# Round 0 of the triangular inverses in blocks of 16, and w_in read 512 columns at a time

## The chip, the cores and the metric

One core of a Trainium2 chip runs the whole program. The metric is the device time of one execution in microseconds (us). The core has a matrix engine (PE), a vector engine (DVE), a scalar engine (ACT), a slower vector engine (POOL) and a sequencer (SP) that issues the DMA transfers. Each engine works through its own instructions in the order in which the program holds them; semaphores make it wait for another engine or for a transfer.

## The reference

Three layers follow each other on 4 sequences of 768 tokens. The first is a delta-rule attention with 8 heads of 48:

```python
for t in range(S):
    y[:, :, t] = einsum('bhd,bhde->bhe', q_t, state)
    v_old = einsum('bhde,bhd->bhe', state, k_t)
    state = state + beta_t * outer(k_t, v_t - v_old)
```

The second is a gated MLP: `h = relu(x @ w_in)`, half of `h` is normalised, mixed over tokens with `w_spatial`, multiplied with the other half, and goes through `w_out`. The third turns that by `theta = x @ w_theta` into `x cos`, `x sin`, mixes each over tokens, adds, and applies `w_ch`. The weights come as 64-bit floats, and `w_in` is 384 x 1024.

## The kernel before

**The recurrence in chunks.** The kernel cuts each sequence into 12 chunks of 64 tokens, 48 chunks in all, which follow each other. Inside a chunk the tokens depend on each other through a strictly lower triangular 64 x 64 matrix per head (the gram matrix of the keys, masked and scaled by beta). With the inverse of one plus that matrix in hand, a chunk is a handful of small matmuls. `chain(g)` emits them: `ru` from the state (L754, L755), a subtraction `rt` on DVE (L758), `ru` again with the inverse from tile `GX` (L765, L766), the new state `s` (L781, L783), and the output `py` (L793, L794). The next chunk needs that state, so the chunks are one long chain.

**The inverses in rounds.** Eight chunks of 4 head pairs make a round: 32 matrices per partition group, inverted together by `invert(r)`. There are six rounds, and two `GX` tiles that take turns. `invert` cuts each 64 x 64 matrix into four 32 x 32 blocks. The two diagonal blocks are turned by a DVE transpose into a layout `un` with one matrix element per column (L624), inverted by substitution, one column `k` at a time from 30 down to 1, a multiply into `tmp` (L646) and an add into `un` (L654) each, and turned back twice, into `xt` (L659) and into `GX` (L662). The off-diagonal block is the product of three: matmuls `f2` (L680) and `f3` (L686) with copies between them, in four groups `h` of 8 matrices (two chunks each). Round 0 cuts the rows of each step into two interleaved halves, so that it has 59 multiplies and 59 adds; the other rounds have 30 and 30. Round r+2 can't start before round r's chunks have used their `GX`.

**The weights.** `f64_to_f32` loads the two 32-bit halves of each number and puts an f32 together with one ACT and four DVE instructions (L815 to L821); `split` makes a high and a low part of it (L827, L828). `load_w1` does this for `w_in` in 12 pieces of 256 columns, whose raw halves lie in buffers of the `vh` ring and whose result lies in the `vl` ring.

**The order.** All instructions are given to a planner (`Plan.run`) as tasks with options of engines, estimated durations, a priority (lower goes first) and dependences. It picks, for each engine, the task that can start first by its estimates, and among equals the one of lower priority; tasks marked `crit` can go ahead of earlier ones. The big matmuls of the MLP (recorded at L895, tile `m`) fill PE between the chain's small ones. So an edit in one place changes the order everywhere behind it.

In the printed functions, `A` adds a task, `pr` is its priority, and `o_dve`, `o_cpp`, `o_cps` and `o_pe` give its engines and estimates.

Of the kernel before, what the change touches and what calls it, by code (L numbers as in the profile page):

```python
# [361 lines left out]
def kernel(  # L362
# [113 lines left out]
    r_un = ring("pa", "un", [128, 32, 32], F32, 1)  # L476
# [17 lines left out]
    load(mask, lambda: mask.t, mask_c, 32768, -58)  # L494
# [117 lines left out]
    def invert(r, pr):  # L612

        gx, G = GXt[r % 2], GXc[r % 2]
        cr = r == 0
# [15 lines left out]
        ub = [Buf(tile_=un.t) for _ in sets]  # L631
        fin = [[] for _ in sets]
        heads = []
        for k in range(30, 0, -1):
            for half in (0, 1):
                for i, (c0, st) in enumerate(sets):
                    t0 = k + 1 + (k + 1 - c0) % st
                    m = len(range(t0, 32, st))
                    if m <= 0:
                        continue  # L640
                    if half == 0:
                        tmp = fin[i] = r_tmp.new()

                        def fa(e, k=k, t0=t0, st=st, m=m, tmp=tmp):
                            t3 = tmp.t[:, 0:m * k].rearrange("p (t s) -> p t s", s=k)
                            eng[e].tensor_tensor(out=t3, in0=un.t[:, k:k + 1, 0:k].to_broadcast([128, m, k]),  # L646
                                                 in1=un.t[:, t0:32:st, k:k + 1].to_broadcast([128, m, k]), op=ALU.mult)

                        dur = d_dve(m * k) if en == "DVE" else d_pool(m * k)
# [688 lines left out]
```

## Time and profile before

| what | value |
|---|---|
| median of 3 runs | 828.1 us (825.38 to 828.17) |
| profiled execution, its own time | 822.64 us |
| its span from first to last instruction | 820.9 us |
| busy share of PE, DVE, ACT, POOL | 89%, 76%, 42%, 20% |
| mean granted TensorE clock | 0.938 of full speed |

A row of the timeline gives the start of an instruction (or of a run of like ones, x their number), its duration, the engine, the source line and the shapes. DVE instructions overlap a little, since the next starts while the last one drains, so the cost of one on a busy DVE is the distance between two starts. A matmul on 32-bit floats is recorded as two passes, so 16 of them show as x32. "idle before" is the time in which the engine stood still, and what it waited for.

### The profile page before, as it was taken

What the parts mean: (1) busy time and instruction counts of PE and PEld (TensorE: products, weight loads), DVE (VectorE), ACT (ScalarE), POOL (GpSimd) and SP (SyncE); (2) the same over time, 40 slices, a digit from 0 to 9 for tenths busy, and PEclk for the clock granted to TensorE, in tenths of its full rate; (3) what the DMA queues carried; (4) which work ended last, traced back from release to release, by engine and by line L of the source; (5) the groups of instructions that cost most, each with busy time, mean ns of one, the idle gap of its engine ahead of it and who ended that gap; (6) DMA issues with size and microseconds to landing.
All of it is one profiled execution on the core that took longest, in us unless ns stands there. A gap on an engine that the chain in (4) does not pass through costs nothing.

```text
span 820.9 us, 21495 instructions
## 1 busy us (share of the span) xinstructions
PE 731.4 (89%) x8672; PEld 672.6 (82%) x8672; DVE 623.4 (76%) x1536; ACT 347.8 (42%) x769; POOL 162.1 (20%) x176
## 2 busy tenths in 40 slices
PE   5256468989999898999999999979999999999998
PEld 5245457777888777897878989979999999999997
DVE  5999998599999899999965574587575575556545
ACT  3536337445534463543754342264333332333321
POOL 2033523143322333401100100042110111111100
PEclk9755769799999999999999999989999999999999
DMA  7615614455577787678684610351021101002001
GB/s 224 207 53 154 192 58 142 119 149 166 154 224 232 208 261 201 174 234 254 185 227 128 213 43 26 109 161 46 26 75 35 27 30 54 27 26 84 1 1 58
DMA packets 84995, 102.39 MB, mean 125 GB/s; under 512 B 8993, under 2 KB 65569, under 8 KB 84897
## 3 DMA queue, kind: packets, MB, share of 16 engines
q1 hardware_dynamic: 84896, 101.03, 41.3%
q8 instruction: 68, 1.11, 0.6%
q14 instruction: 31, 0.25, 0.1%
HBM read 74.38 MB, written 22.41 MB: 118 GB/s over the span
## 4 chain that ended last, share of the span: by engine, by line
PE 57%; DVE 24%; DMA 10%; issue 3%; ACT 3%; SPq 2%; POOLq 0%; ACTq 0%; DVEq 0%
PE m L895 30%; PE y L895 19%; DVE tmp L646 5%; DVE un L654 4%; DMA xr<-xd 2%; DMA xd<-xs 2%; PE gp L588 2%; SPq L431 2%; DMA vk<-in_vkn_dram 2%; PE ru L765 1%; PE py L793 1%; DMA k<-in_vkn_dram 1%; DVE GX L599 1%; DMA kq<-pp 1%; PE m L1181 1%
## 5 line engine op out<-in xcount | busy, mean ns | idle before, releaser
L895 PE MATMUL m<-w,vh 128*128 128x256 f32 x576 | 111.1, 292 | 0.7 <-ACT uT L401 0.5
L895 PEld LDWEIGHTS m<-w,vh 128*128 128x128 f32 x576 | 89.0, 191 | 4.3 <-ACT uT L401 0.7
L895 PE MATMUL y<-wr,z 128*128 128x384 f32 x432 | 88.1, 343 | 0.0
L895 PE MATMUL y<-w,z 128*128 128x384 f32 x432 | 84.6, 339 | 0.0
L895 PE MATMUL m<-w,vl 128*128 128x256 f32 x288 | 81.2, 282 | 0.0
L895 PEld LDWEIGHTS y<-wr,z 128*128 128x128 f32 x432 | 77.3, 191 | 0.0
L895 PEld LDWEIGHTS y<-w,z 128*128 128x128 f32 x432 | 75.6, 188 | 0.0
L646 DVE TENSOR_TENSOR tmp<-un 128x30 f32<-128x30 f32 (+21 forms) x209 | 68.5, 339 | 0.8
L654 DVE TENSOR_TENSOR un<-un,tmp 128x30 f32<-128x30 f32 (+21 forms) x209 | 66.9, 331 | 0.9
L765 PE MATMUL ru<-rt,GX 64*64 64x48 f32 x384 | 34.8, 235 | 34.2 <-DVE rt L758 33.9
L765 PEld LDWEIGHTS ru<-rt,GX 64*64 64x64 f32 x384 | 28.6, 146 | 43.3 <-DVE rt L758 39.6
L1201 DVE TENSOR_SCALAR ni<-m 128x384 int32<-128x384 f32 x24 | 13.3, 555 | 57.6 <-PE m L895 57.5
L895 PEld LDWEIGHTS m<-w,vl 128*128 128x128 f32 x288 | 54.9, 191 | 0.0
L566 POOL TENSOR_TENSOR gm<-mask,ng 128x256 f32<-128x256 f32 x53 | 40.7, 774 | 53.6 <-DVE pp L609 18.5
L895 PE MATMUL m<-wo,gh 128*128 128x384 f32 x192 | 48.9, 335 | 1.6 <-DVE rr L1203 1.6
L730 POOL TENSOR_TENSOR vk<-vk,ng 128x384 f32<-128x384 f32 x28 | 28.6, 1024 | 104.8 <-DMA vk<-in_vkn_dram 72.9
L895 PE MATMUL m<-xTh,wih 128*128 128x256 f32 x144 | 46.6, 323 | 0.0
L401 ACT ACTIVATE x<-m 128x384 f32<-128x384 f32 x15 | 7.3, 488 | 86.9 <-PE m L895 86.9
L401 ACT ACTIVATE W<-ru 64x192 f32<-64x192 f32 x85 | 27.5, 324 | 36.4 <-PE ru L766 35.0
L895 PE MATMUL m<-xTl,wih 128*128 128x256 f32 x144 | 41.2, 286 | 0.0
L895 PE MATMUL m<-xTh,wil 128*128 128x256 f32 x144 | 41.0, 285 | 0.0
L588 PE MATMUL gp<-kg 48*64 48x128 f32 x512 | 38.1, 291 | 2.4 <-issue 2.4
(189 smaller groups left out, 2070.4 us busy)
## 6 DMA issues: line engine op xcount, KB each, us to landing
kq<-in_kqT_dram SPq DMA_DIRECT2D x96, 128.0 KB, 3.8
vk<-in_vkn_dram SPq DMA_DIRECT2D x48, 192.0 KB, 3.5
kg<-in_kqT_dram SPq DMA_DIRECT2D x32, 256.0 KB, 3.4
gd<-gt SPq DMA_DIRECT2D x24, 256.0 KB, 3.6
graw<-gd SPq DMA_DIRECT2D x24, 256.0 KB, 2.8
k<-in_vkn_dram SPq DMA_DIRECT2D x24, 192.0 KB, 3.1
xd<-xs SPq DMA_DIRECT2D x48, 96.0 KB, 2.8
xr<-xd SPq DMA_DIRECT2D x24, 192.0 KB, 3.3
```

What stands on the lines that cost most here:

```text
L401: nc.scalar.activation(out=out, in_=in_, func=func, **kw)
L431: return P.add(dma(nbytes), lambda e: nc.sync.dma_start(out=out_fn(), in_=src), reads, [(buf, part)], prio, extra=LOADLAT)
L566: eng[e].tensor_tensor(out=gm.t, in0=mask.t.unsqueeze(1).to_broadcast([128, HP, CH]), in1=ng_b[r].t[:, j, 1].unsqueeze(2).to_broadcast([12 ...
L588: mm(out=pv()[o:o + 64, hp, :], lhsT=kh, rhs=kg.t[i:i + D, :, hp, :] if fused else kh, start=True, stop=True)
L599: nc.vector.scalar_tensor_tensor(out=GXt[1][:, u0 + hp], in0=GXt[1][:, u0 + hp], scalar=ng_b[1].t[:, j, 1, hp:hp + 1], in1=mask.t, op0=ALU ...
L646: eng[e].tensor_tensor(out=t3, in0=un.t[:, k:k + 1, 0:k].to_broadcast([128, m, k]), in1=un.t[:, t0:32:st, k:k + 1].to_broadcast([128, m, k ...
L654: eng[e].tensor_tensor(out=un.t[:, t0:32:st, 0:k], in0=un.t[:, t0:32:st, 0:k], in1=t3, op=ALU.add)
L730: lambda e: eng[e].tensor_tensor(out=vk.t, in0=vk.t, in1=ng_b[r].t[:, j].unsqueeze(3).to_broadcast([128, 2, HP, D]), op=ALU.mult), [ng_b[r ...
L765: mm(out=pu.t[64:128, hp, :], lhsT=gx[64:128, u, :], rhs=rt.t[64:128, hp, :], start=True, stop=True)
L793: mm(out=PYt[0:48, hp, q:q + 64], lhsT=w[:, 0, hp, :], rhs=kq.t[:, 1, hp, :], start=True, stop=True)
L895: mm(out=view(), lhsT=a, rhs=c, start=(start and q == 0 and s_ == 0), stop=(stop and q == tot - 1 and s_ == 2))
L1201: P.add(o_dve(DM), lambda e: nc.vector.tensor_scalar(out=ni.t, in0=th(), scalar1=1.0 / TWO_PI, scalar2=None, op0=ALU.mult), [ps], [ni], pr ...
```

## The change

1. **Substitution in blocks of 16, round 0 alone** (`TWO = (0,)`). The steps run from k = 14 down to 1, on the two 16 x 16 diagonal blocks of each 32 x 32 block at once: one multiply and one add per step, 28 instructions. The interleaved halves are gone in round 0 too; each instruction follows the one before.
2. **The block between them by products.** Each 32 x 32 block then needs its own off-diagonal 16 x 16 block. For each of the four groups, 32 small matmuls `g1` (L692) multiply, ACT copies the result to `ct` with a scale of 0 or 1 per partition, 64 small matmuls `g2` (L698, L700) multiply again, and two DVE instructions `s1`, `s2` (L711, L715) merge the results into `GX` and `xt`. The zeros and ones are two new columns of the mask tile. `g1` and `g2` use a PSUM buffer of the ring `m`.
3. **Groups one after another.** In round 0 each group of two chunks has its own copies (L722) and its own clearing (L725, POOL), and the later three groups get priorities 0.4, 2.4 and 4.4, which stand just ahead of the chunks that need them.
4. **w_in in 6 pieces of 512 columns**, whose raw halves lie in the buffers of the `uT` ring.

```diff
-    r_un = ring("pa", "un", [128, 32, 32], F32, 1)
+    r_un = ring("pa", "un", [128, 33, 32], F32, 1)
...
-        sets = [(0, 1)] if not cr else [(0, 2), (1, 2)]
...
+        if two:
+            ub = (lambda: un.t.rearrange("p t s -> p (t s)").rearrange("p (b x) -> p b x", b=2)[:, :, 0:512]
+                  .rearrange("p b (t s) -> p b t s", s=32))
+        for k in range(14 if two else 30, 0, -1):
+            m = (15 if two else 31) - k
+            tmp = r_tmp.new()
+            n = m * k * (2 if two else 1)
+            def fa(e, k=k, m=m, tmp=tmp, n=n):
+                if two:
+                    u4, t4 = ub(), tmp.t[:, 0:n].rearrange("p (b t s) -> p b t s", b=2, s=k)
+                    eng[e].tensor_tensor(out=t4, in0=u4[:, :, k:k + 1, 0:k].to_broadcast([128, 2, m, k]),
+                                         in1=u4[:, :, k + 1:16, k:k + 1].to_broadcast([128, 2, m, k]), op=ALU.mult)
+                    return
...
+            A([(en, dur)], fa, [un], [tmp], pr + 0.001 * (31 - k), crit=cr)
+            A([(en, dur)], fb, [tmp], [un], pr + 0.001 * (31 - k), crit=cr)
...
+        step = MU if two else 32
+        for h0 in range(0, 32, step):
+            p1 = pr + 0.2 if h0 == 0 else r * RM + h0 / HP + GH
...
+                    def g1(e, v1=v1, u0=u0):
+                        for u in range(MU):
+                            for q in (0, 32, 64, 96):
+                                mm(out=v1()[q:q + 32, u, :], lhsT=gx[q:q + 16, u0 + u, 0:32], rhs=xt.t[q:q + 16, u0 + u, :],
+                                   start=True, stop=True, tile_position=(q, q))
+                    def g2(e, v2=v2, u0=u0, ct=ct):
+                        for u in range(MU):
+                            for q in (0, 32, 64, 96):
+                                mm(out=v2(0)[q:q + 32, u, :], lhsT=ct.t[q:q + 32, u, :], rhs=gx[q:q + 32, u0 + u, 16:32],
+                                   start=True, stop=True, tile_position=(q, q))
+                                mm(out=v2(1)[q:q + 32, u, :], lhsT=gx[q:q + 32, u0 + u, 0:32], rhs=ct.t[q:q + 32, u, 0:16],
+                                   start=True, stop=True, tile_position=(q, q))
+                    A(o_pe(620), g1, [xt, gu], [ps], p1, crit=cr, act=0.185, mode=3)
+                    A([("ACT", d_actp(32 * MU))], lambda e, v1=v1, ct=ct: act(ct.t, v1(), ACTF.Copy, scale=mask_t.t[:, CH + 1:CH + 2]),
+                      [ps, mask_t], [ct], p1, crit=cr, port=False)
+                    A(o_pe(1150), g2, [ct, gu], [(ps, True)], p1, crit=cr, act=0.2, mode=3)
...
+                    A(o_dve(16 * MU), s1, [ps, gu, mask_t], [un1], p1, crit=cr, port=False)
+                    A(o_dve(16 * MU), s2, [ps, xt, mask_t], [xn1], p1, crit=cr, port=False)
...
-    r_cvr = Ring(pools, "pm", [128, 256, 2], I32, "vh", 6)
+    r_cvr = Ring(pools, "pm", [128, DF, 2], I32, "uT", 3)
...
-                for c in (c0, c0 + 256):
-                    pr = (WP0 + 0.1 * n) if n < 6 else 0.5 + 0.3 * n
+                pr = (WP0 + 0.1 * n) if n < 3 else 0.5 + 0.6 * n
```

**How the order moves.** Three places in the engines' order follow. The first is DVE at the end of round 0's substitution. `un` is the layout with one element per column, `GX_108` round 0's matrices, `vl` a piece of w_in. Before, the last steps, the two transposes back and what follows:

```order
L646 TENSOR_TENSOR tmp<-un 128x30
L654 TENSOR_TENSOR un<-un,tmp 128x14x2
L654 TENSOR_TENSOR un<-un,tmp 128x15x2
L646 TENSOR_TENSOR tmp<-un 128x15 x2
L654 TENSOR_TENSOR un<-un,tmp 128x15 x2
L659 STREAM_TRANSPOSE xt_725<-un 128x32x32
L662 STREAM_TRANSPOSE GX_108<-un 128x32x32
L407 COPY GX_108<-GX_108 32x32x32
```

Now the same place:

```order
L643 TENSOR_TENSOR tmp<-un 128x52
L653 TENSOR_TENSOR un<-un,tmp 128x2x13x2
L643 TENSOR_TENSOR tmp<-un 128x28
L653 TENSOR_TENSOR un<-un,tmp 128x2x14
L667 STREAM_TRANSPOSE xt_571<-un 128x32x32
L665 STREAM_TRANSPOSE GX_108<-un 128x32x32
L542 TENSOR_SCALAR ss<-ss 128x32
L767 TENSOR_TENSOR kq<-gp,gm 64x256 x2
```

In the whole substitution 118 instructions became 28, the multiplies and adds now alternate, and the copy of `GX` no longer follows the transposes.

The second place is PE behind these transposes. `mg` and `m` are PSUM tiles, `ru` the chain's. Before, from the first `f2` (L680) to chunk 0 (L765):

```order
L680 MATMUL mg<-xt_725,GX_108 32x32 x16
L686 MATMUL mg<-GX_108,ct 32x32 x16
L680 MATMUL mg<-xt_725,GX_108 32x32 x16
L765 MATMUL ru<-rt,GX_108 64x48
L766 MATMUL ru<-rt,GX_108 64x48
```

Now, from the last of `g2`'s rows (L698, L700; 128 of these matmuls stand here one by one, behind a row of 64 of L692) to chunk 0 (L820):

```order
L698 MATMUL m<-GX_108,ct 32x16
L700 MATMUL m<-ct,GX_108 32x16
L735 MATMUL mg<-xt_571,GX_108 32x32 x16
L692 MATMUL m<-xt_571,GX_108 32x32 x32
L741 MATMUL mg<-GX_108,ct 32x32 x16
L692 MATMUL m<-xt_571,GX_108 32x32 x32
L820 MATMUL ru<-rt,GX_108 64x48
L821 MATMUL ru<-rt,GX_108 64x48
```

So 64 `g1` and 128 `g2` matmuls (two groups) stand ahead of the first `f2`, and the `g1` of the other two groups ahead of chunk 0.

The third place is DVE ahead of round 1's substitution, which works on `GX_109`. Before:

```order
L599 SCALAR_TENSOR_TENSOR GX_109<-GX_109,ng,mask 128x64 x12
L712 TENSOR_TENSOR kq<-gp,gm 64x256
L599 SCALAR_TENSOR_TENSOR GX_109<-GX_109,ng,mask 128x64 x20
L817 TENSOR_SCALAR vl<-vl 128x256 x2
L819 SCALAR_TENSOR_TENSOR vl<-vh,vl 128x256 x2
L535 TENSOR_REDUCE ss<-k 128x8
L821 SCALAR_TENSOR_TENSOR vl<-vh,vl 128x256
L535 TENSOR_REDUCE ss<-k 128x8
L407 CAST wih_135<-vl 128x256
L821 SCALAR_TENSOR_TENSOR vl<-vh,vl 128x256
L758 TENSOR_TENSOR rt<-ru,vk 128x192
L828 TENSOR_TENSOR wil_138<-vl,wih_135 128x256
```

Now:

```order
L711 SCALAR_TENSOR_TENSOR GX_108<-GX_108,mask,m 128x8x16
L715 SCALAR_TENSOR_TENSOR xt_571<-xt_571,mask,m 128x8x16
L409 COPY GX_108<-GX_108 32x8x32
L602 SCALAR_TENSOR_TENSOR GX_109<-GX_109,ng,mask 128x64 x24
L711 SCALAR_TENSOR_TENSOR GX_108<-GX_108,mask,m 128x8x16
L715 SCALAR_TENSOR_TENSOR xt_571<-xt_571,mask,m 128x8x16
L409 COPY GX_108<-GX_108 32x8x32
L409 COPY GX_109<-GX_109 32x32x32
L767 TENSOR_TENSOR kq<-gp,gm 64x256 x2
L627 STREAM_TRANSPOSE un<-GX_109 128x1024
```

The w_in rows and chunk 1's `rt` that stood between the scaling of `GX_109` and round 1's transpose now stand behind that transpose, and the merges `s1` and `s2` of two groups stand ahead of it.

## Rows read from the trace of the kernel before

**Rows 1.** Page part 2, 40 slices of 20.5 us: busy tenths, granted clock
```profile
DVE  5999998599999899999965574587575575556545
PEclk9755769799999999999999999989999999999999
```

**Rows 2.** Windows: start:end, length, busy (x) of PE, PEld, DVE, ACT, POOL, PEclk, DMA
```profile
20.00:40.00 20.00, 6.03 (x104) 5.47 (x100) 19.45 (x100) 12.01 (x41) 0.00 (x0) 0.74 0.72 218
40.00:60.00 20.00, 10.32 (x256) 9.20 (x256) 19.61 (x58) 7.26 (x18) 8.03 (x9) 0.50 0.20 54
80.00:100.00 20.00, 11.84 (x155) 9.84 (x152) 19.66 (x50) 8.11 (x19) 11.53 (x13) 0.72 0.70 194
100.00:120.00 20.00, 10.54 (x123) 8.57 (x118) 19.92 (x65) 4.51 (x12) 5.91 (x7) 0.57 0.28 80
120.00:140.00 20.00, 18.28 (x475) 15.97 (x475) 17.65 (x43) 14.60 (x33) 7.98 (x11) 1.00 0.41 122
600.00:700.00 100.00, 100.00 (x584) 99.64 (x583) 61.15 (x116) 34.38 (x71) 12.11 (x10) 1.00 0.14 46
```

**Rows 3.** Timeline of DVE, round 0: first multiply, last adds, two transposes back
```profile
22.89 0.18 DVE L646 TENSOR_TENSOR tmp<-un 128x30 f32<-128x30 f32 x1
42.83 0.30 DVE L654 TENSOR_TENSOR un<-un,tmp 128x15 f32<-128x15 f32 x2
43.17 1.97 DVE L659 STREAM_TRANSPOSE xt<-un 128x1024 f32<-128x1024 f32 x1
45.03 1.86 DVE L662 STREAM_TRANSPOSE GX<-un 128x1024 f32<-128x1024 f32 x1
```

**Rows 4.** Timeline of DVE, round 2: steps with nothing between them
```profile
160.14 0.27 DVE L646 TENSOR_TENSOR tmp<-un 128x108 f32<-128x108 f32 x1
160.44 0.27 DVE L654 TENSOR_TENSOR un<-un,tmp 128x108 f32<-128x108 f32 x1
```

**Rows 5.** Timeline of DVE: w_in at 256 columns; round 1's first transpose and first back
```profile
63.47 0.74 DVE L819 SCALAR_TENSOR_TENSOR vl<-vh,vl 128x256 int32<-128x256 int32 x2
69.52 1.94 DVE L624 STREAM_TRANSPOSE un<-GX 128x1024 f32<-128x1024 f32 x1
121.22 2.11 DVE L659 STREAM_TRANSPOSE xt<-un 128x1024 f32<-128x1024 f32 x1
```

**Rows 6.** Groups by form, 40 to 75 us: busy us, mean ns, idle before
```profile
L599 DVE SCALAR_TENSOR_TENSOR GX<-GX,ng,mask 128x64 f32<-128x64 f32 x32 | 9.1, 354 | 0.0
L401 ACT ACTIVATE ct<-mg 32x256 f32<-32x256 f32 x6 | 2.3, 375 | 12.5 <-PE mg L680 12.5
```

**Rows 7.** Timeline of PE: f2 in round 0, chunk 0's start, f2 in round 1
```profile
45.19 1.06 PE L680 MATMUL mg<-xt,GX 32*32 32x32 f32 x32 [18.72 <-DVE xt L659]
51.09 0.34 PE L765 MATMUL ru<-rt,GX 64*64 64x48 f32 x1
123.93 0.69 PE L680 MATMUL mg<-xt,GX 32*32 32x32 f32 x32
```

**Rows 8.** Timeline of DVE: `rt` of chunk 1 and of chunk 5
```profile
65.93 0.34 DVE L758 TENSOR_TENSOR rt<-ru,vk 128x192 f32<-128x192 f32 x1
119.61 0.34 DVE L758 TENSOR_TENSOR rt<-ru,vk 128x192 f32<-128x192 f32 x1
```

**Rows 9.** Windows of 5 us, chunks 8 and 9; columns as in rows 2
```profile
140.00:145.00 5.00, 3.24 (x86) 2.96 (x88) 2.98 (x8) 3.12 (x8) 0.61 (x1) 0.74 0.51 155
145.00:150.00 5.00, 5.00 (x88) 4.38 (x84) 0.84 (x2) 2.44 (x7) 0.61 (x1) 0.50 0.33 84
150.00:155.00 5.00, 5.00 (x74) 4.46 (x73) 1.81 (x5) 2.63 (x3) 0.61 (x1) 0.74 0.59 184
```

**Rows 10.** Chain that ended last, in order of time: start, us, what
```profile
92.00 1.90 PE gp L588 x16
121.00 1.09 PE gp L588 x16
451.49 41.31 PE m L895 x294
```

More of the change, by code (lines that the diff above doesn't have):

```diff
@@ L57 @@
 POOL_ROUNDS = ()
+TWO = (0,)
+GH = -1.6
 DYN = ("gp", "gm", "m")
@@ L493 @@
     load(beta_sb, lambda: beta_sb.t, beta, 128 * 768, -59)
[L494 removed]
+    load(mask, lambda: mask.t, mask_c, 33792, -58)
     for i in range(2):
@@ L615, in invert @@
         cr = r == 0
+        two = r in TWO
         gg = [Buf(tile_=gx) for _ in range(4)]
-        gz = [Buf(tile_=gx) for _ in range(4)]
         for q in (1, 3):
@@ L628, in invert @@
         en = "POOL" if r in POOL_ROUNDS else "DVE"
-        sets = [(0, 1)] if not cr else [(0, 2), (1, 2)]
[L631 to L649, printed above, removed]
-                        heads.append(A([(en, dur)], fa, [un, ub[i]], [tmp], pr + 0.001 * (31 - k), crit=cr))
-                    else:
-                        def fb(e, k=k, t0=t0, st=st, m=m, tmp=fin[i]):
-                            t3 = tmp.t[:, 0:m * k].rearrange("p (t s) -> p t s", s=k)
-                            eng[e].tensor_tensor(out=un.t[:, t0:32:st, 0:k], in0=un.t[:, t0:32:st, 0:k], in1=t3, op=ALU.add)
-                        dur = d_dve(m * k) if en == "DVE" else d_pool(m * k)
-                        A([(en, dur)], fb, [fin[i], un], [ub[i]], pr + 0.001 * (31 - k), crit=cr).order.update(heads[-3:])
@@ new lines, in invert, with back @@
+        xt = r_xt.new()
+        gu = Buf(tile_=gx)
+        def back(e):
+            nc.vector.transpose(out=gx[:, :, 0:32].rearrange("p u t -> p t u"), in_=un.t[:, 0:32])
+        tr = [lambda: A([("DVE", 1900.0)], lambda e: nc.vector.transpose(out=xt.t.rearrange("p u s -> p s u"),
+                                                                         in_=un.t[:, 0:32].rearrange("p t s -> p s t")),
+                        [un], [xt], pr + 0.05, crit=cr, port=False),
+              lambda: A([("DVE", 1900.0)], back, [un], gg + [gu], pr + 0.1, crit=cr, port=False)]
@@ L664, in invert @@
+        for f in tr[::-1] if two else tr:
+            f()
         if cr:
             inv0.append(P.tasks[-1])
-        for q in (1, 3):
-            A(o_cps(1024), lambda e, q=q: copy(e, gx[32 * q:32 * q + 32, :, 32:64], gx[32 * q:32 * q + 32, :, 0:32]),
-              [], [gg[q]], pr + 0.2, crit=cr, part=32 * q)
-        for q in (1, 3):
-            A([("POOL", 890.0)], lambda e, q=q: nc.gpsimd.memset(gx[32 * q:32 * q + 32, :, 0:32], 0.0),
-              [gg[q]], [gz[q]], pr + 0.3, crit=cr, port=False)
@@ L932, in m_V @@
               for kk in range(KX)]
-        wr = [x for kk in range(KX) for c in (2, 3) for x in wiq[kk, c]]
+        wr = [x for kk in range(KX) for x in wiq[kk, 1]]
         mm_tasks(ps, lambda: ps.t, gr, DF, [hi, lo] + wr, pr)
@@ L986, in m_U @@
                   for kk in range(KX)]
-            wr = [x for kk in range(KX) for x in wiq[kk, f // 2]]
+            wr = [x for kk in range(KX) for x in wiq[kk, 0]]
             mm_tasks(ps, lambda ff=ff: v3()[:, ff, :], gr, TG, [hi, lo] + wr, pr, per=UPER)
```

116 lines of the change are left out of this document (75 added, 41 removed).

## The prediction

> **What bounds the kernel now.** I read the two slice rows of the page first, to find the stages [rows 1]. From slice 2 to slice 7 (about 20 to 125 us) DVE stands at 8 to 9 tenths while the clock granted to PE is mostly 5 to 7 tenths. From slice 8 on the clock is full or nearly so. The windows say the same in numbers [rows 2]: from 20 to 120 us DVE is busy 19.5 to 19.9 of every 20 us, PE only 6.0 to 11.8, and those at a mean clock of 0.50 to 0.74. From 120 us PE is busy 18.3 of 20 at full clock, and from 600 to 700 us it never stops. So up to some 120 us DVE sets the pace and PE loses most of its time; behind that PE is the bound, except for a dip at 140 to 155 us [rows 9]. The last big stretch of the chain of waits before the second layer's end is 41.31 us of nothing but big matmuls [rows 10]: whatever the recurrence leaves over is worked off there at full rate. A change that brings everything at 120 us forward by some time brings the end forward by the same, if PE's later work is neither longer nor more broken.
>
> **The change part by part.**
>
> *Substitution.* Before, it lasts from 22.89 to 43.17 us, 20.3 us [rows 3], with two reductions of the norms (about 0.5 us each) among its steps. Now there are 28 instructions, sizes 28 to 112 and back, 2240 elements in all, 80 on average. No other row stands between most of them, and each waits for the one before. Such a pair starts 0.30 us apart at 108 elements [rows 4]. Between a 30-element step (0.18) [rows 3] and a 108-element step (0.27) [rows 4] an element costs 1.15 ns, so 80 elements take 0.30 - 28 x 0.00115 = 0.27 us. 28 x 0.27 = 7.5, with the reductions 8.5. Gain 20.3 - 8.5 = 11.8 us. The new operands have one dimension more, which the trace doesn't show; if each instruction cost 0.30 throughout, the gain is 10.9, and if it overlapped like independent ones (0.20), 13.7.
>
> *Merges and copies, added on DVE.* Eight merges of 128 elements with one operand in PSUM. The nearest row is the scaling with a per-partition scalar, 64 elements, 9.1 / 32 = 0.28 us each [rows 6], and an upper end is its mean duration of 0.354 with 64 elements more, 0.43. I take 0.30: +2.4 (2.2 to 3.4). Two copies of 1024 columns become copies by group; those that fall to DVE cost at most 4 x 0.28 = 1.1 and one goes, so +0.5.
>
> *w_in.* Six pieces fewer with five DVE instructions each: 30 fewer, the elements as before. Two at 256 columns take 0.74, 0.37 each [rows 5]; the elements are 256 x 1.15 ns = 0.295, which leaves 0.075 that an instruction costs by itself. 30 x 0.075 = 2.2 us gained, 0 if the wide ones wait longer on transfers twice as large. I take -2.2. Four DVE rows of w_in and chunk 1's `rt` also move behind round 1's first transpose; that changes when round 1 starts, and not when it ends.
>
> *Sum on DVE up to the end of round 1's substitution:* -11.8 + 2.4 + 0.5 - 2.2 = -11.1 us. Round 1's first transpose back, at 121.22 us [rows 5], should come at about 110. Its own start, at 69.52, comes forward by more: the 11.1 and about 5 us of moved w_in rows.
>
> *PE's new work and the wait in front of it.* The trace has no four-way tiled products. The nearest row is `f2`: 16 matmuls, 32 passes, 1.06 us at half clock and 0.69 at full [rows 7]. PE has then stood still for 18.72 us, so half clock holds. By passes, `g1` of a group (64) costs 2.1 us and `g2` (128) 4.2; if four row tiles ran side by side where `f2` has two, half that. Ahead of the first `f2` now stand `g1` and `g2` of two groups: 6.4 to 12.7 us, and two more `g1` ahead of chunk 0, of which some 1 us hides in the copies to `ct` (0.375 each [rows 6]). Chunk 0 began 51.09 - 46.9 = 4.2 us behind the transposes [rows 3, 7]. Now the transposes end at 46.9 - 11.8 = 35.1, and chunk 0 begins at 35.1 + 4.2 + 6.4 + 1 = 46.7 at best, 35.1 + 4.2 + 12.7 + 3.2 = 55.2 at worst: between 4 us earlier and 4 us later. I take 50, towards the price by passes, since that is what a row shows. This wait costs little by itself, because DVE has 12 us of scalings, norms and w_in to do that don't need it; its first merge, though, stands ahead of 24 scalings and waits for `g2` of its group. By passes this is at 35.1 + 4.2 + 4.2 = 43.5, and the rows of DVE ahead of that merge (norms, 8 scalings, reductions, w_in) last till about 42. So 0 to 2 us are lost there, and I add nothing. The other groups' `g2` come between the early chunks, where PE is idle about half of the time [rows 2], and cost DVE and the end nothing.
>
> The Trainium skill weighs in on the price of `g1` and `g2`: "TensorE: Matmul & The Clock Gate", section "Part 3: Packing small matmuls — row/col tiling", says that matmuls on different 32-row strips run concurrently in the array. No row here shows four strips. By that rule the lower price holds and chunk 0 comes near 47 us; by passes near 55. Neither changes the sum on DVE.
>
> *What is late next.* In the new order of DVE the chunks move less than the inverse. Chunk 1's `rt` (65.93) and chunk 5's (119.61) [rows 8] now stand behind more of round 1's steps; by the rows between them I put chunk 5 at about 112, 7 us earlier, and round 1's end 11 us earlier. The filler work of PE needs both the chunks' outputs and w_in, which is converted earlier too. So what reaches the end lies between 7 and 11 us from this, and up to 9 us more if DVE's stillness of 140 to 155 us (15 - 2.98 - 0.84 - 1.81 = 9.4 us [rows 9]) goes, which the order suggests: round 1's `f2` and `f3` now stand ahead of chunk 7 and not of chunk 8, and round 2's first transpose comes fewer rows behind. I take the 11.1 of the sum: span 820.9 - 11.1 = 809.8, execution 822.64 - 11.1 = 811.5. That profiled execution is 5.5 us faster than the median of the runs shown, 828.1; against that median the forecast is 828.1 - 11.1 = 817 us.
>
> **The rivals.**
>
> *A, the gain stays in the front.* The inverse is ready early, but the chunks are what feeds PE, and they come at the pace of `g1`, `g2` and of the DVE rows queued ahead of each `rt`. For it: chunk 0 may come later than before, and the later groups' products, merges, clearing on POOL and copies stand in the chain of chunks 1 to 6, where before one transposition served all. Against it: DVE is full up to 120 us, and its work shrinks. It would give a gain of 0 to 4 us: about 826.
>
> *B, more than the sum.* With round 1's inverse ahead of chunk 7, the dip at 140 to 155 us disappears as well: 11.1 + 9.4 = 20 us, 808. For it: in that dip DVE waits [rows 9] for work that the chunks bring. Against it: PE is busy all of 145 to 155 us, only at a clock of 0.50 and 0.74; if PE does the same work there, only the clock can be won back, some 3.5 us.
>
> *C, slower.* In the new order the big matmuls are used up early: 63 of them stand ahead of chunk 7 and still 63 ahead of chunk 10 (before 45 and 72). With nothing to fill in, PE runs the chunks' small matmuls alone, and may do so at half clock: a group of 16 passes of the gram matmul takes 1.90 us at half and 1.09 at full [rows 10], a difference of 0.8, and a chunk has about four such groups and `jit`'s, so some 3.3 us per chunk. The gain of 11.1 is gone after 3.4 chunks at half clock on the path; with 7 (chunks 5 to 11) the kernel is 12 us slower, 840. For it: at 145 to 150 us PE is busy 5.00 of 5 us and still granted only 0.50 [rows 9]. Against it: the stretch of 120 to 140, also made of small matmuls, kept full clock [rows 2], and chunks that run alone are earlier for it, with the fillers left for later. The Trainium skill ("TensorE: Matmul & The Clock Gate", section "HAM oscillation — how this bites in real kernels") describes bursts between waits that each start at half rate; the window of 145 to 150 us agrees with it, and by that rule C is where the time would go.
>
> **How the numbers follow.** Forecast (the sum on DVE reaches the end, 7 to 14 us gained, 814 to 821): 0.55. B: 0.18. A: 0.18. C: 0.09. The range reaches from B to A, 806 to 826. A difference under 0.5%, 4.1 us, is about what a measurement of this kernel can't tell from none; so faster takes the forecast, B and about a third of A less the tail of the forecast: 0.78. Same takes most of A: 0.13. Slower: C, 0.09.
>
> **What would show each step right or wrong.** On DVE, the substitution of round 0 should last 8 to 9 us and its 28 steps start about 0.27 us apart, and round 1's first transpose back should start at 108 to 112 us. On PE, `g1` of a group should take 1.1 to 2.1 us at half clock, and chunk 0 start at 47 to 55 us. Chunk 5's `rt` at 112, and the stretch of pure big matmuls before the second layer's end, 41 us before, longer, since the chunks run ahead of the fillers. The mean clock should stay at 0.93 or more. The prediction is wrong if round 1's inverse comes early and the windows from 120 us on show PE waiting or at 0.50 for over 10 us more than before (C), or if chunk 5 is no earlier than 119 us (A).

## The result: slower by 1.3%, though the front comes earlier

The changed kernel takes 837.8 us (833.98 to 838.96, 4 runs) beside 826.7 us of the kernel before on the same chip: ratio 1.013, 95% interval 1.008 to 1.018. Run again later beside other kernels (e5 below) it gave 1.0135 (1.009 to 1.018). The forecast was 817 us. Executions more than 1.5% above the fastest of the same kernel are left out of the medians and ratios below; e15 has two of them among four, and so no ratio.

The profiled execution took 833.98 us, with a span of 832.2 us and a mean granted clock of 0.914. The two slice rows of its page, as in [rows 1] (a slice is now 20.8 us):

```profile
DVE  5999966998998999898578664487584574557545
PEclk9755658688999999979999999999999999999999
```

DVE's first gap, two slices at 6 tenths, is the sixth and seventh slice (104 to 146 us). The clock, which before stood at 9 in every slice but one from the ninth on, is at 5 in the sixth slice and at 6 to 8 from there to the tenth (208 us). DVE's timeline first, against [rows 3, 5, 8]: first multiply of round 0, its two transposes back, round 1's first transpose in and first back, and `rt` of chunks 5 and 6:

```profile
23.01 0.18 DVE L643 TENSOR_TENSOR tmp<-un 128x28 f32<-128x28 f32 x1
32.36 1.99 DVE L667 STREAM_TRANSPOSE xt<-un 128x1024 f32<-128x1024 f32 x1
34.24 1.88 DVE L665 STREAM_TRANSPOSE GX<-un 128x1024 f32<-128x1024 f32 x1
...
51.85 1.95 DVE L627 STREAM_TRANSPOSE un<-GX 128x1024 f32<-128x1024 f32 x1
...
105.77 1.93 DVE L667 STREAM_TRANSPOSE xt<-un 128x1024 f32<-128x1024 f32 x1
...
110.82 0.34 DVE L813 TENSOR_TENSOR rt<-ru,vk 128x192 f32<-128x192 f32 x1
...
128.79 0.36 DVE L813 TENSOR_TENSOR rt<-ru,vk 128x192 f32<-128x192 f32 x1 [2.10 <-PE ru L810]
```

Round 0's substitution lasts 9.35 us and not 20.3, round 1's inverse comes back 15.4 us earlier (105.77 for 121.22), chunk 5's `rt` 8.8 us earlier (110.82 for 119.61). Then the gain goes within one chunk: chunk 6's `rt` is at 128.79, where the kernel before has it at 126.16. Part of it returns and goes again: chunk 10's is at 159.33 for 165.47, chunk 16's at 208.17 for 206.33, the last at 451.5 for 447.8. The timeline of PE shows where it starts: first `g1`, chunk 0's `fu` (the `ru` matmuls with the inverse), the last big matmul ahead of round 1's first `f2`, and that `f2`:

```profile
36.27 1.93 PE L692 MATMUL m<-xt,GX 16*32 16x32 f32 x128 [9.63 <-DVE ss L542]
...
52.27 0.31 PE L820 MATMUL ru<-rt,GX 64*64 64x48 f32 x1 [0.33 <-ACT GX L403]
...
104.59 0.39 PE L949 MATMUL m<-wih,xTl 128*128 128x512 f32 x1
107.84 0.34 PE L735 MATMUL mg<-xt,GX 32*32 32x32 f32 x11 [2.86 <-DVE xt L667]
```

Round 1's first `f2` now stands on PE ahead of chunk 5's `fu`, and waits 2.86 us for the transpose `xt` that was brought forward. Windows of 5 us around it (columns as in [rows 2]):

```profile
100.00:105.00 5.00, 4.59 (x42) 3.19 (x42) 4.62 (x15) 2.71 (x6) 1.28 (x2) 1.00 0.59 158
105.00:110.00 5.00, 2.15 (x54) 1.98 (x56) 4.97 (x7) 0.49 (x1) 0.00 (x0) 0.82 0.02 3
110.00:115.00 5.00, 5.00 (x85) 4.59 (x82) 3.85 (x14) 2.85 (x7) 3.07 (x4) 0.50 0.22 56
115.00:120.00 5.00, 5.00 (x47) 4.13 (x45) 2.61 (x6) 2.00 (x5) 1.84 (x2) 0.50 0.15 35
120.00:125.00 5.00, 5.00 (x106) 4.52 (x103) 2.28 (x8) 2.15 (x6) 1.05 (x2) 0.50 0.36 110
125.00:130.00 5.00, 5.00 (x71) 4.71 (x71) 2.48 (x6) 1.87 (x4) 0.64 (x2) 0.50 0.58 159
130.00:135.00 5.00, 5.00 (x96) 4.32 (x93) 2.10 (x6) 1.61 (x5) 0.98 (x2) 0.79 0.29 98
```

At full clock until 105 us, idle for most of 105 to 110, and then, in the windows from 110 to 130 us, PE never stops and is granted 0.50, which is 1.2 of its 2.4 GHz (in windows of 1 us, from 108 to 132). DVE is now the one that stands still: busy 2.1 to 3.9 of each 5 us from 110 us on. The same windows of the kernel before, from 120 us on, run at full clock [rows 2]. It happens again at 155 to 165 us and 185 to 190 us (0.50) and, in parts, between 325 and 375 us, where in a row of PE's waits `ru` waits for `rt` four times between 300 and 400 us:

```profile
PE ru L820 <- DVE rt L813: 7.1, 4, 2.8
```

(columns: us in total, times, longest). The kernel before has 1.2 us of that in the same stretch.

**An account of PE's time.** From 125 us on PE is the bound, so what counts is the time that it stands still, and the busy time that half clock takes from it, which is busy time x (1 - clock). Two windows of the kernel before, which no rows above show, then of the changed kernel:

```profile
125.00:300.00 175.00, 161.46 (x2905) 137.23 (x2903) 155.53 (x410) 87.57 (x194) 52.10 (x62) 0.96 0.62 181
300.00:500.00 200.00, 193.50 (x2783) 169.04 (x2780) 159.89 (x411) 97.75 (x216) 32.02 (x29) 0.99 0.61 179
```

```profile
125.00:300.00 175.00, 162.06 (x2824) 139.17 (x2822) 155.28 (x385) 73.87 (x173) 50.33 (x61) 0.90 0.61 177
300.00:500.00 200.00, 188.91 (x2677) 165.60 (x2678) 160.44 (x391) 95.08 (x213) 36.24 (x34) 0.95 0.62 182
```

Before: idle 13.5 + 6.5, half clock 161.46 x 0.04 + 193.50 x 0.01 = 8.4, together 28.4 us. Changed: idle 12.9 + 11.1, half clock 162.06 x 0.10 + 188.91 x 0.05 = 25.7, together 49.7. So 21.2 us more are lost behind 125 us, and the span is 11.3 us longer. The 9.9 us between the two I call head start; they are what the account leaves over, and were not measured. About twice that was lost behind it.

### The profile page after: what moved, and what is told of

Its sections match the earlier page's. It is cut to its first block, busy times and chain, and to the rows that moved or that the text cites. A ratio compares the mean times of both kernels' runs of the same rounds, so it can differ in the third digit from the quotient of the medians.

```text
span 832.2 us, 22936 instructions
## 1 busy us (share of the span) xinstructions
PE 758.6 (91%) x9440; PEld 699.2 (84%) x9440; DVE 623.1 (75%) x1423; ACT 342.9 (41%) x764; POOL 171.0 (21%) x186
## 4 chain that ended last, share of the span: by engine, by line
PE 59%; DVE 24%; DMA 7%; issue 4%; ACT 2%; SPq 2%; POOLq 0%; ACTq 0%; DVEq 0%
PE m L949 31%; PE y L949 17%; DVE tmp L647 4%; DVE un L656 4%; DMA bgr<-in_w_r_dram 2%; PE py L848 2%; DMA vk<-in_vkn_dram 2%; PE ru L820 2%; PE gp L591 2%; PE ru L809 1%; SPq L433 1%; PE s L836 1%; PE mg L735 1%; PE m L1235 1%; PE mg L741 1%
## 5 line engine op out<-in xcount | busy, mean ns | idle before, releaser
L949 PEld LDWEIGHTS m<-w,vh 128*128 128x128 f32 x576 | 90.9, 195 | 4.4 <-ACT uT L403 1.5
L656 DVE TENSOR_TENSOR un<-un,tmp 128x30 f32<-128x30 f32 (+9 forms) x150 | 58.0, 387 | 1.0
L647 DVE TENSOR_TENSOR tmp<-un 128x30 f32<-128x30 f32 (+9 forms) x150 | 56.4, 376 | 1.1
L820 PEld LDWEIGHTS ru<-rt,GX 64*64 64x64 f32 x384 | 30.1, 153 | 30.1 <-DVE rt L813 21.9
L820 PE MATMUL ru<-rt,GX 64*64 64x48 f32 x384 | 36.3, 242 | 20.6 <-DVE rt L813 20.3
L949 PE MATMUL m<-xTh,wih 128*128 128x256 f32 x144 | 48.4, 336 | 0.0
L569 POOL TENSOR_TENSOR gm<-mask,ng 128x256 f32<-128x256 f32 x53 | 37.2, 709 | 54.4 <-DVE pp L612 25.1
L591 PE MATMUL gp<-kg 48*64 48x128 f32 x512 | 41.7, 312 | 2.3 <-DVE kq L767 1.6
L949 PE MATMUL m<-xTh,wil 128*128 128x256 f32 x144 | 42.7, 296 | 0.0
L949 PE MATMUL m<-wt,xh 128*128 128x384 f32 x144 | 37.1, 339 | 2.8 <-ACT xh L403 2.8
```

What stands on the lines that cost most here:

```text
L569: eng[e].tensor_tensor(out=gm.t, in0=mask.t[:, 0:CH].unsqueeze(1).to_broadcast([128, HP, CH]), in1=ng_b[r].t[:, j, 1].unsqueeze(2).to_broa ...
L591: mm(out=pv()[o:o + 64, hp, :], lhsT=kh, rhs=kg.t[i:i + D, :, hp, :] if fused else kh, start=True, stop=True)
L656: eng[e].tensor_tensor(out=un.t[:, k + 1:32, 0:k], in0=un.t[:, k + 1:32, 0:k], in1=t3, op=ALU.add)
L820: mm(out=pu.t[64:128, hp, :], lhsT=gx[64:128, u, :], rhs=rt.t[64:128, hp, :], start=True, stop=True)
L949: mm(out=view(), lhsT=a, rhs=c, start=(start and q == 0 and s_ == 0), stop=(stop and q == tot - 1 and s_ == 2))
```

## The experiments

All ratios are to the kernel before, run beside it on the same chip. e1 to e4, e5 to e8, e9 to e12 and e13 to e16 were run together, so a difference between two groups is less sure than one within a group.

| kernel | median us | ratio | 95% interval |
|---|---|---|---|
| e1 w_in at 512 alone | 830.26 | 1.0051 | 1.0015 to 1.0088 |
| e2 blocks alone | 830.38 | 1.0070 | 1.0032 to 1.0108 |
| e3 changed, 28 fillers | 829.99 | 1.0045 | 1.0004 to 1.0087 |
| e4 changed, 116 fillers | 824.57 | 1.0004 | 0.9962 to 1.0045 |
| e5 changed | 837.63 | 1.0135 | 1.0092 to 1.0178 |
| e6 changed, 4 us | 818.12 | 0.9897 | 0.9852 to 0.9942 |
| e7 changed, 2 us | 831.16 | 1.0076 | 1.0033 to 1.0119 |
| e8 before, 48 fillers | 831.63 | 1.0078 | 1.0045 to 1.0112 |
| e9 before, other order | 835.12 | 1.0104 | 1.0062 to 1.0146 |
| e10 before, other order | 834.97 | 1.0117 | 1.0072 to 1.0162 |
| e11 before, 72 fillers | 826.61 | 1.0024 | 0.9991 to 1.0057 |
| e12 changed, 28 elsewhere | 836.98 | 1.0139 | 1.0090 to 1.0187 |
| e13 before, 4 us | 846.97 | 1.0272 | 1.0196 to 1.0349 |
| e14 before, 2 us | 838.53 | 1.0159 | 1.0088 to 1.0230 |
| e15 changed, 3 us | 835.62 | none | none |
| e16 changed, 6 us | 826.74 | 1.0025 | 0.9976 to 1.0074 |

**e1 and e2: the two parts alone.** e1 is the kernel before with w_in in 512 columns; e2 is the changed kernel with w_in in 256, so the blocks alone:

```diff
-                for c in (c0, c0 + 256):
-                    pr = (WP0 + 0.1 * n) if n < 6 else 0.5 + 0.3 * n
...
+                pr = (WP0 + 0.1 * n) if n < 3 else 0.5 + 0.6 * n
```

That is e1 against the kernel before; e2 against the changed kernel is the same edit the other way round.

> The kernel before with one part of the change: w_in in 6 pieces of 512 columns, round 0's substitution as before. Clock theory (the loss is PE running at half clock where round 0's shorter substitution lets small work come early): no loss here, 0 to 3 us faster than before, since 30 DVE instructions go, and the clock cost, PE's busy time at less than full rate, stays near the 30 us that I work out for the kernel before. Rival, that the wide pieces upset the order (transfers twice as large in a ring of 3): most of the 11 us loss shows here, 8 us or more slower than before.

> The changed kernel with w_in back in 12 pieces of 256 columns, so the blocks of 16 alone. Clock theory: round 1's first transpose back again near 106 to 110 us, a stretch of PE busy at half clock behind it, and a time 5 to 15 us above before. Rival, that w_in is the cause: within 4 us of before or faster.

Measured: each alone is slower, by 0.5% and 0.7%. e1 lies between its two theories. In e2 round 1's inverse comes back earlier than expected, in e1 later than in the kernel before (the first transpose back, e1 and then e2):

```profile
123.94 2.11 DVE L659 STREAM_TRANSPOSE xt<-un 128x1024 f32<-128x1024 f32 x1
100.22 2.04 DVE L667 STREAM_TRANSPOSE xt<-un 128x1024 f32<-128x1024 f32 x1
```

The half clock that I expected behind it in e2 is not there. PE keeps full clock from 100 to 135 us, of which two windows:

```profile
105.00:110.00 5.00, 5.00 (x67) 3.84 (x66) 3.17 (x10) 3.77 (x9) 3.23 (x4) 1.00 0.15 39
125.00:130.00 5.00, 5.00 (x92) 4.81 (x90) 1.59 (x4) 0.97 (x4) 0.61 (x1) 1.00 0.58 167
```

Still the end is later: in the account above e2's execution loses 16.1 us more behind 125 us than the kernel before, and e1 13.1. So neither part is the one that fails, shorter work in front does not by itself shorten the whole, and the wait at 105 us is not the only way to lose it.

**e3 and e4: filler matmuls in the waits.** The order stays that of the changed kernel; 128 x 128 x 256 matmuls whose result nobody reads stand in PE's waits. e3: 28 ahead of round 1's first `f2`. e4: also 28, 8, 28 and 24 ahead of `fu` of chunks 9, 10, 31 and 33.

```diff
                 def f2(e, ps=ps, u0=u0):
+                    warmup(WARM2.get((r, u0), 0))
...
         def fu(e):
+            warmup(WARMU.get(g, 0))
...
+    def warmup(n):
+        for _ in range(n):
+            mm(out=MGt[:, MU:2 * MU].rearrange("p a b -> p (a b)"), lhsT=wi_h[0].t[:, DF:DF + 128], rhs=wi_h[0].t[:, DF:DF + 256],
+               start=True, stop=True)
```

> The changed kernel, its order untouched, with 28 matmuls of 128x256 whose result nobody reads put on PE just ahead of round 1's first f2, where PE stood still for 2.86 us at 105 us and its clock fell to half for the 25 us that followed. Clock theory: the clock stays full from 105 to 135 us, the 13 us of busy time lost there to half clock come back to the end but for 1 us: 9 to 13 us faster than the changed kernel, about 826. Rival, that the new order itself (waits on DVE, more small matmuls) costs the time and the clock only goes along with it: the dummies cost their 3 us or nothing, 0 to 4 us slower than the changed kernel.

> As the kernel with 28 dummy matmuls, and dummies also ahead of the inverse's matmul of chunks 9 (28), 10 (8), 31 (28) and 33 (24), where PE of the changed kernel waited for DVE at 150, 159, 328 and 351 us and then ran at half clock. Clock theory: another 5 to 12 us faster than with the first 28 alone, 815 to 821, below the kernel before. Rival (order): no faster than the first 28 alone, or slower by the dummies' up to 10 us.

Measured: 1.0045 and 1.0004, where the changed kernel without them has 1.0135. Windows of e3, which answer to those of the changed kernel above:

```profile
105.00:110.00 5.00, 5.00 (x66) 4.64 (x64) 4.87 (x9) 0.00 (x0) 0.30 (x1) 1.00 0.02 6
110.00:115.00 5.00, 4.79 (x121) 4.18 (x117) 3.99 (x9) 2.51 (x5) 2.66 (x4) 1.00 0.22 56
115.00:120.00 5.00, 4.62 (x134) 3.97 (x129) 4.70 (x14) 4.61 (x13) 2.48 (x3) 1.00 0.34 95
120.00:125.00 5.00, 5.00 (x107) 4.52 (x105) 4.61 (x15) 1.62 (x4) 2.25 (x4) 1.00 0.52 139
```

The wait is filled, the clock stays at 1.00, chunk 6's `rt` is at 123.3 us for 128.8 and chunk 16's at 198.5 for 208.2. The order of the work is the same, so what the filler gives back is the clock: half clock behind that wait cost the end some 7 us (0.9% of 825; by the two intervals 2 to 12), less than the 9 to 13 expected. With the other four waits filled it is some 3 less again, where I expected 5 to 12; the intervals of e3 and e4 can't tell that from nothing. In the account e3 has 10.5 us less half clock than the changed kernel, but 9.1 us more idle time, so not every us of clock comes back at the end. e4 in the two windows of the account:

```profile
125.00:300.00 175.00, 159.43 (x2852) 135.53 (x2848) 161.30 (x404) 76.47 (x179) 50.96 (x61) 0.98 0.64 187
300.00:500.00 200.00, 192.56 (x2699) 170.88 (x2696) 155.64 (x380) 97.15 (x214) 34.65 (x31) 1.00 0.58 171
```

Lost: idle 15.6 + 7.4, half clock 3.2, 26.2 us, 2.2 fewer than before. But 88 of its fillers stand there, and cost up to 88 x 0.124 = 10.9 us of PE themselves (the price of one is from e8). That is why it only reaches the kernel before.

**e5 to e7: the wait filled with work that is due anyway.** e5 is the changed kernel once more. In e6 the planner is told that round 1's `xt` can be used 4 us later, in e7 2 us later:

```diff
+XE = 4000.0
...
-                        [un], [xt], pr + 0.05, crit=cr, port=False),
+                        [un], [xt], pr + 0.05, crit=cr, port=False, extra=XE if r == 1 else 0.0),
```

> The changed kernel, unchanged, on the chip and in the session of the next three, since its first times come from another session than the kernels with filler matmuls. Theory (TensorE's clock: a new wait in front of round 1's first f2 lets it fall to half for 25 us, and again at 155, 185 and 330 us): the ratio to before is again about 1.013, chunk 6's rt near 129 us and chunk 16's near 208. Rival (any other order of the planner costs about half a per cent, and the first ratio of 1.013 was high by the session): 1.004 to 1.007, as for w_in alone (1.005) and the blocks alone (1.007).

> The changed kernel; the planner is told that round 1's xt can be used 4 us later than it thinks, so it puts 34 pieces of big matmuls ahead of round 1's first f2 and not 30: work that has to be done anyway stands in the wait. No work is added. Theory (clock): PE is not idle at 105 to 108 us, the granted clock stays up there, chunk 6's rt comes near 124 us (129 in the changed kernel), chunk 16's near 199 (208), and the ratio to before is about 1.003 (0.998 to 1.007), some 1% under the changed kernel. Rival (order luck): chunk 6 still near 129, and the time anywhere within 0.7% of the changed kernel's.

> The control of that edit: 2 us in place of 4. The planner still puts 30 pieces ahead of round 1's first f2, so the wait stays, though the order behind it is another (28 of 32 later places differ in what stands ahead of them). Theory (clock): PE is idle some 2 to 3 us in front of that f2 and works at half clock behind it, chunk 6 near 128 us, ratio to before 1.008 to 1.014. Rival (order luck): no tie to that wait; a ratio under 1.005 is as likely as one above 1.01.

Measured: e5 repeats the result. e6 is faster than both kernels, 0.9897. Its PE in front of that `f2`, and the windows:

```profile
107.86 0.40 PE L950 MATMUL m<-wih,xTl 128*128 128x512 f32 x1
...
111.79 0.28 PE L950 MATMUL m<-xTh,wil 128*128 128x256 f32 x1
112.00 0.69 PE L736 MATMUL mg<-xt,GX 32*32 32x32 f32 x32
```

```profile
105.00:110.00 5.00, 5.00 (x63) 3.90 (x63) 4.87 (x9) 0.50 (x1) 0.55 (x1) 0.74 0.11 41
110.00:115.00 5.00, 3.97 (x89) 3.39 (x85) 4.76 (x11) 1.87 (x4) 2.80 (x4) 1.00 0.39 105
115.00:120.00 5.00, 4.07 (x89) 3.52 (x89) 4.59 (x18) 3.72 (x8) 1.27 (x3) 1.00 0.14 40
120.00:125.00 5.00, 3.43 (x91) 2.96 (x92) 4.81 (x10) 3.08 (x8) 1.93 (x3) 1.00 0.57 149
```

No wait is shown at that `f2`, and PE is at full clock from 110 us on (in the window before it had begun at half). Chunk 6 is at 124.5 us, chunk 16 at 194.3, forecast 199; the ratio is below the 0.998 that was forecast, so the order behind that `f2` gained something as well. e7, the control, keeps the wait:

```profile
107.63 0.54 PE L736 MATMUL mg<-xt,GX 32*32 32x32 f32 x23 [2.31 <-DVE xt L668]
```

and half clock behind it, but for some 10 us and not 24 (0.50 in 110 to 115, 0.56 in 115 to 120, then 1.00), with chunk 6 at 122.1 where I expected 128. Its ratio of 1.0076 lies just under the range expected. So the wait in front of that `f2` brings the clock down each time it is there (2.86 us in the changed kernel, 2.78 in e5, 2.31 here); how long it stays down depends on what follows, and I can't say from these traces on what of it.

**e8 and e11: the same filler in the kernel before.** e8: 36 ahead of chunk 4's `fu` and 12 ahead of round 1's last `f2`. e11: 72 ahead of chunk 4's `fu` and none elsewhere.

```diff
+WARM2 = {(1, 24): 12}
+WARMU = {4: 36}
```

e11 has `{}` and `{4: 72}` in these two lines.

> The kernel before, its order untouched, with filler matmuls whose result nobody reads: 36 in PE's wait of 8.79 us in front of chunk 4's fu (109.28 us) and 12 in the wait of 2.00 us in front of round 1's last f2 (141.76 us). Theory (clock): in the kernel before too the clock is what is lost there; the 10 us from 109 to 119 us run at full clock, chunk 5's rt comes near 114 us (119.6), the stretch at half clock from 143 to 153 us goes, and the end comes 5 to 10 us earlier: ratio 0.988 to 0.994. Rival (up to 121 us the substitution on DVE sets the pace, and PE's clock costs nothing that the end sees): chunk 5 earlier, round 1's end at 121 as before, chunk 8 and the ratio unchanged, 0.998 to 1.004.

> The kernel before with 72 filler matmuls in front of chunk 4's fu, and none elsewhere. With 36 of them PE had still stood 4.29 us in front of it and the clock had fallen again, so that try did not test what it was meant to. 72 at 0.124 us each last 8.9 us, as long as the wait. Theory (clock): full clock from 109 to 120 us, where before had half; chunk 5's rt near 115 us (119.6), round 1's end still at about 121 us, since DVE sets it; the 9 big matmuls and those behind come some 3 to 5 us earlier, and the end 0 to 4 us: ratio 0.995 to 1.000. Rival (PE's clock in front of 120 us costs the end nothing): 0.999 to 1.004.

e8 missed its aim. Its filler and the `fu` behind it:

```profile
100.09 4.57 PE L865 MATMUL mgt<-wih 128*128 128x256 f32 x36
108.95 0.34 PE L771 MATMUL ru<-rt,GX 64*64 64x48 f32 x1 [4.29 <-DVE rt L763]
```

36 took 4.57 us at full clock (about 0.124 each), and the rest of the wait brought the clock down as before: 0.50 at 110 to 115 us. It ended 0.8% slower, with 9.9 us more lost in the account, and so did not test the clock. e11 did:

```profile
110.00:115.00 5.00, 4.80 (x100) 4.16 (x101) 4.28 (x14) 1.60 (x5) 0.44 (x1) 1.00 0.10 33
115.00:120.00 5.00, 2.72 (x27) 1.94 (x21) 4.97 (x21) 0.83 (x2) 2.11 (x2) 1.00 0.39 112
```

```profile
119.57 0.34 DVE L763 TENSOR_TENSOR rt<-ru,vk 128x192 f32<-128x192 f32 x1
121.18 2.09 DVE L663 STREAM_TRANSPOSE xt<-un 128x1024 f32<-128x1024 f32 x1
```

Full clock from 110 to 120 us, and yet chunk 5's `rt` is at 119.57 (119.61 before) and not at the 115 I expected, and the ratio is 1.0024. In the kernel before DVE sets the pace up to 121 us, and half clock there costs the end nothing: the rival was right. In the changed kernel DVE is no longer full from 110 us on, and the same half clock costs.

**e12: the filler where PE doesn't wait.** The changed kernel, with the 28 ahead of chunk 19's `fu` (`WARMU = {19: 28}`, `WARM2 = {}`).

> Control of the filler: the changed kernel with the 28 filler matmuls in front of chunk 19's fu (235 us), where PE is busy 6.00 of 6 us at full clock and waits for nothing. Theory (filler helps only where it stands in a wait that would bring the clock down): chunk 6's rt near 129 and chunk 16's near 208 as in the changed kernel, and 28 x 0.124 = 3.5 us more: ratio to before about 1.017 (1.012 to 1.022). Rival (filler moves the time by some other way, such as where it shifts the order of waits): near the 1.0045 that the same 28 gave in front of round 1's f2.

Measured: 1.0139, chunk 6 at 127.7 and chunk 16 at 208.9 us, as in the changed kernel. Filler helped only in the wait. Its own 3.5 us are inside the interval. e12 is also the fair comparison for e3's profile: both were granted 1.00 from 20 to 100 us, where the changed kernel had 0.50 to 0.74, and e12 still falls to half behind the wait:

```profile
115.00:120.00 5.00, 5.00 (x69) 4.38 (x70) 2.77 (x7) 1.88 (x4) 2.30 (x2) 0.50 0.20 54
```

**e9 and e10: the kernel before in another order.** Not a line of the work differs, only a priority of the planner:

```diff
-WP0 = 0.6
+WP0 = 0.7
```

That is e9; e10 sets `NPR` to 0.6 in place of 0.5.

> The kernel before with the same work in another order: one priority in the planner (w_in's first piece, WP0) is 0.7 in place of 0.6, and from the front of the program on PE and DVE come in another order. Nothing of the change is in it. Theory (PE's clock and waits behind 120 us depend on the order as a whole, and the kernel before has a good one): slower than before by 0.3 to 1%, as w_in alone (1.005) and the blocks alone (1.007) were, with more idle time or half clock in 300 to 400 us than before's 6 us. Rival (w_in alone and the blocks alone lost by what they themselves do): within 0.3% of before.

> A second order of the same work: the priority of the norms (NPR) is 0.6 in place of 0.5. Theory (order as a whole): slower than before by 0.3 to 1%, or, if orders scatter evenly around before, somewhere else within 1% of it; in either case the ratio follows idle time plus half clock behind 120 us. Rival (parts lose by what they do): within 0.3%.

Measured: 1.0104 and 1.0117, just above the 0.3 to 1% expected and nearly the loss of the changed kernel. So an order alone can cost what the change cost.

**e13 to e16: five orders of each kernel.** The edit of e6 in the kernel before (4 and 2 us), and with 3 and 6 us in the changed one.

> The kernel before with the edit of e6: the planner is told that round 1's xt can be used 4 us later than it thinks. Theory one (the change is worth its 11 us at equal luck of the order; the kernel before has a good order, and other orders of it lose about 1%): 1.006 to 1.014. Theory two (that edit helps by itself, with or without the change): 0.987 to 0.995, as e6.

> The kernel before with the edit of e7, 2 us. Theory one: 1.004 to 1.014. Theory two: within 0.5% of before on either side.

> The changed kernel with 3 us: as with 2 us, 30 pieces of big matmuls stand ahead of round 1's first f2. Theory one: orders with the change scatter around a mean that is about 1% under the mean of orders without it, so 0.990 to 1.008. Theory two: 1.007 to 1.015, as the changed kernel and e7. By the wait in front of that f2 alone, which stays, it would be slower than e6.

> The changed kernel with 6 us: 35 pieces and chunk 5's fu stand ahead of round 1's first f2, so the wait is filled, or turned round (that f2 is late and round 1 with it). Theory one: 0.988 to 1.003. Theory two: 1.007 or more.

Measured: in the kernel before the edit costs 2.7% and 1.6%, so it is no gain by itself (theory two falls), and both are above the ranges of theory one. The edit tells the planner something that isn't so, which may cost by itself; e9 and e10 are free of that. With 6 us the changed kernel is level with the kernel before, inside the range. Its wait has only moved, from the `f2` to chunk 5's `fu`, with 0.50 behind it from 115 to 120 us:

```profile
112.20 0.25 PE L821 MATMUL ru<-rt,GX 64*64 64x48 f32 x1 [3.10 <-DVE rt L814]
```

e15 keeps a wait of 1.70 us at that `f2`, with half clock behind it. Its two times that count, 832.07 and 839.16 us, are 0.7% and 1.6% over the kernel before (825.98): one in the range and one outside it, which settles nothing. The account for all orders, worked out from the same two windows of each as above (us; differences to the kernel before; the last column is span less loss):

| kernel | idle | half clock | lost more | span longer | rest |
|---|---|---|---|---|---|
| e10 before, other order | 28.7 | 16.5 | 16.8 | 12.7 | -4.1 |
| e14 before, 2 us | 24.3 | 21.8 | 17.7 | 15.9 | -1.8 |
| e9 before, other order | 26.9 | 24.4 | 22.9 | 14.0 | -8.9 |
| e13 before, 4 us | 25.8 | 33.3 | 30.7 | 22.8 | -7.9 |
| e6 changed, 4 us | 21.2 | 18.3 | 11.1 | -3.6 | -14.7 |
| e16 changed, 6 us | 22.8 | 17.3 | 11.7 | 1.7 | -10.0 |
| e7 changed, 2 us | 29.3 | 15.7 | 16.6 | 4.4 | -12.2 |
| changed | 24.0 | 25.7 | 21.2 | 11.3 | -9.9 |
| e15 changed, 3 us | 29.0 | 26.6 | 27.2 | 16.4 | -10.8 |

Within either kernel the span follows what PE loses behind 125 us. Every other order loses more than the kernel before, whose 28.4 us are the fewest of all these orders. The rest is a mean of -5.7 us without the change and -11.5 with it: at equal loss the change is some 6 us ahead. But each row comes from one execution, which can lie 4 to 6 us off its kernel's median (the one of the kernel before, 822.64 us, is 4 us under), and by the same account e1 has a rest of -7.3 us and e2, the blocks alone with the earliest inverse of all, -3.7; so the 6 us are no measure of what the change is worth. As times: five orders without the change have ratios of 1.000 to 1.027, mean 1.013; five with it 0.990 to 1.014 (e15 by its two times, 1.012), mean 1.005. The difference is smaller than the scatter. That the change gains at equal luck of the order is not shown.

## Why the prediction was wrong

*The sum on DVE* had the right sign and was 4.3 us short: round 1's inverse came back 15.4 us earlier for 11.1, at 105.77 for the 108 to 112 forecast, and chunk 5 at 110.82 for 112. Its largest term held: the substitution took 9.35 us for 8.5. From the third step on its steps start 0.28 us apart on average, for 0.27 taken, and a wait of 0.69 us for ACT in front of a reduction makes most of the rest. The parts, however, don't add up as summed. The blocks alone, 8.9 us of the sum, bring the inverse back 21.0 us earlier (e2), and w_in alone, 2.2 us of it, 2.7 us later (e1). So which rows the planner puts ahead of round 1's end counts as much as the terms, and that the total came out near is in part luck.

*The price of `g1` and `g2`* lay just under the lower end: `g1` of two groups took 1.93 us at half clock, 0.97 each, for 1.1 to 2.1 forecast, and its 128 passes took under half of what as many of `f2`'s would (32 in 1.06 us [rows 7]). The Trainium skill ("TensorE: Matmul & The Clock Gate", section "Part 3: Packing small matmuls — row/col tiling") has matmuls on different strips run concurrently; this row agrees. Chunk 0 began at 52.27, inside the 47 to 55.

*The failed step* is "A change that brings everything at 120 us forward by some time brings the end forward by the same, if PE's later work is neither longer nor more broken", of which I took the condition for granted when I carried "the 11.1 of the sum" to the span. It was more broken: 4.0 us more idle and 17.3 us more half clock behind 125 us. I had read the order around round 1's end for which rows come earlier, and not asked whether the `f2` that moved ahead of chunk 5's `fu` would find its `xt` ready. It did not, by 2.86 us, and 24 us at half clock followed. e3 shows what that wait was worth: 0.9% of the time, of a total error of 2.5%. The rest is put down to the later waits and their half clock by the account alone; e4, with four of these filled, doesn't settle their price.

*Rival C* had the sign and nearly the size (840 for 837.8) but not its trigger. The mark that the prediction set for it, over 10 us more of waiting or 0.50 from 120 us on, is met. It had the big matmuls run out; in fact they were left over: the pure stretch of them behind the chunks grew from the 41.31 us of [rows 10] to

```profile
454.45 49.12 PE m L949 x363
```

The forecast also had it grow, but by chunks that run ahead, and the last chunk came 3.7 us later. What brought the clock down was a wait of PE for DVE with big matmuls queued behind the waiting instruction. Nor did the work behind such a wait start at half clock: `f2` at 141.76 us of the kernel before took 0.69 us, the price at full clock, and the clock fell some 0.6 us after its start; in e5 it fell 2.4 us after. My point against C, that 120 to 140 us kept full clock, was a property of the order before and not of the work. Its chance of 0.09 was too small for another reason as well: e9, e10, e13 and e14 show that four new orders of the kernel before, with nothing of the change in them, lost 1.0 to 2.7%. The kernel before is not a typical order of its work, and I weighed the change as if the new order would be as good.

*Rival A* fell with chunk 5, *B* with the windows of 110 to 135 us, though e6, the best of five orders, shows that one exists in which the change gains 1.0%, near the 1.3% forecast.

## What to carry to other kernels

When a planner orders the instructions, one build of a change measures the change and the luck of its order together; run several orders on both sides before you judge, and where all four new orders of an unchanged kernel lose, as here, expect the first build of a change to lose as well. When an edit makes something ready earlier, look in the new order at who now stands in front of it and waits: a wait of 3 us on PE cost some 7, because the work behind it ran at half clock. Half clock cost the end nothing where DVE set the pace (e11), so account for it where PE is the bound: idle time plus busy time x (1 - clock), stage by stage, against the same account of the kernel before.

## What the hardware showed that I had not expected

From 110 to 130 us PE was busy 5.00 of every 5 us and stayed at 0.50, with small f32 matmuls and bursts of three to nine big ones. Nine big ones at 124.4 to 126.7 us did not bring the clock back; it rose while nine ran at 130.4 to 132.5, and in the kernel before while nine others ran at 115.7 to 119.3. What makes the difference is open. The granted clock of the first 100 us differs between executions of one order without any effect on what comes out: from 20 to 100 us e12 was granted 1.00 and the changed kernel 0.50 to 0.74, with the same order up to there, and chunk 4's `rt` is at 96.5 and 96.4 us. So the mean clock of an execution says little, and the 0.93 of the forecast was no test: the kernel before took 825.75 us at a mean clock of 0.925 and 825.45 us at 0.965. And filler that ends 4.29 us before the work arrives (e8) did not hold the clock, whereas filler up to the end of the wait did (e3, e11).
